# Merging VectorE calls in a convolution ahead of a GELU MLP, and leading with four short token blocks in place of six

## The chip, the cores and the metric

The kernel runs on one core of a Trainium2 chip. The metric is the time of one execution in device microseconds (us), taken as the median of several executions. The granted TensorE clock is the mean of a whole run. In four runs (two of the kernel before, one each of runs 2 and 4) it was 0.999 at ordinary times, and these count as undisturbed; a run at 1.000 or 0.999 is called clean.

## The reference, cut to what matters

A causal depthwise convolution of seven taps (softmax weights, one set for each of eight groups of 24 channels) is followed by a two-layer MLP with an exact GELU. Everything is float32 outside, bfloat16 in the matmuls.

```python
# x (8, 4096, 192), weight (8, 7), w_in (192, 2048), w_out (2048, 192)
w = softmax(weight, axis=-1)
x_pad = concat([zeros(B, 6, D), x], axis=1)          # causal: six zeros ahead of each sequence
a[b, s, c] = sum_k w[c // 24, k] * x_pad[b, s + k, c]
h = a.reshape(32768, 192) @ w_in
out = gelu_exact(h) @ w_out
```

## The kernel before

The 32768 tokens are two halves of 16384, worked on together; a block is so many tokens of both halves. `WS` gives the block sizes. For each block the following happens:

- SyncE loads the input into one of three buffers `xin`.
- VectorE transposes it to channel-major form (`xT`; 192 channels of two halves are three parts of 128 rows) and runs seven taps over it. The last tap writes `xc` in bfloat16.
- TensorE multiplies by `w_in` (here mm1) in slices: eight slices for a 256-token block, sixteen for one of 512. Each slice fills one of two PSUM buffers `hp`.
- ScalarE applies the GELU to a slice and frees its `hp` buffer. So TensorE can be two slices ahead of ScalarE, no more.
- TensorE multiplies the GELU's output of the block before by `w_out` (mm2), a share after each slice of mm1.

Blocks 0 and 1 are convolved on TensorE. For the blocks in `K0`, ScalarE takes the first tap (a scaled copy), at the slices that `first` names; it needs the transposed block for that. TensorE's program order is mm1 slice, mm2 share, mm1 slice, and so on, without any slack.

```python
    WS = [256] * 6 + [512] * ((HALF - 1536) // 512)
    PC = {0: 0, 1: 1}                # convolved on TensorE
    K0 = {4: 0, 5: 1, 6: 2}          # first tap on ScalarE
    NA = 5                           # blocks whose output ScalarE evacuates
    M0, M1 = 6, NB - 1               # first and last block of the transposed mm2
# ... (cut)
            def trans(n, p):                       # VectorE, part p of block n
                # ... waits for the input, for xT to be free, for the halo
                v.transpose(
                    ap(xT[n % 2], p * XW + HX, [[NP * XW, 128], [1, w]]),
                    ap(xin[n % NX], p, [[TB // 32 * DQ, 128], [D if n == 0 else DQ, w // 32], [NP, 32]]),
                ).then_inc(S_TR)

            def conv(n, k, p):                     # VectorE, tap k of part p
                # ... waits
                if k == h and h:
                    v.wait_ge(S_K0, NP * K0[n] + p + 1)
                elif idx >= NP:
                    v.wait_ge(S_CV, idx - NP + 1)
                src = ap(xT[n % 2], p * XW + HF + kt, [[NP * XW, 128], [1, w]])
                a = acc[n % 2][:, p * TB : p * TB + w]
                # k == 0: tensor_scalar; else scalar_tensor_tensor(dst, src, wk, a, mult, add)

            for n in range(2, NB):                 # VectorE's order
                ops = [] if n in K0 else [("t", n, p) for p in range(NP)]
                ops += [("c", n, k, p) for k in range(int(n in K0), KS) for p in range(NP)]
                if n + 1 in K0:
                    ops[9:9] = [("t", n + 1, p) for p in range(NP)]
                plan.append(ops)
# ... (cut) ScalarE
            for n, at in ((4, (3, 5, 6)), (5, (3, 5, 6)), (6, (2, 3, 5))):
                for p in range(NP):
                    first[n - 2, at[p]] = (n, p)   # ahead of slice at[p] of block n - 2
            for n in range(NB):
                for i in range(NSL[n]):
                    if (n, i) in first:
                        first_tap(*first[n, i])    # waits for S_TR of that part
                    for k in due.get((n, i), []):
                        evac(a, *k)
                    a.wait_ge(S_MM1, u + 1)        # u counts slices over all blocks
                    a.activation(out=..., in_=hp[u % 2], func=AF.Gelu).then_inc(S_GELU)
# ... (cut) TensorE
            def mm1(n, i):
                if u >= 2:
                    t.wait_ge(S_GELU, u - 1)       # the hp buffer is free
                if i == 0:                         # (blocks 0 and 1 wait for other semaphores: cut)
                    t.wait_ge(S_CV, cvd(n))        # the whole block is convolved
```

## Time and profile before

| | before |
|---|---|
| time, median of 4 runs | 682.59 us (682.43 to 682.80) |
| span of the profiled run, clock | 680.6 us, 1.000 |
| VectorE: busy, calls | 561.7 us, 906 |
| VectorE waiting for TensorE at the output transpose | 99.9 us |
| TensorE from block 4's first slice to block 6's (two short blocks) | 49.91 to 70.95 us |

TensorE is the bound (busy for 99% of the span, 98% of the chain of waits). The timeline of each engine gives the start of every call, and the difference of two starts is what a call costs its engine. The lines are in the prediction.

### The profile page before, as it was taken

To read this page: it belongs to the slowest core of one execution; us is meant where nothing else is said; L and a number is where in the kernel's file an instruction comes from. 1 tells how busy PE (TensorE), PEld (TensorE's weight loads), DVE (VectorE), ACT (ScalarE), POOL (GpSimd) and SP (SyncE) were. 2 spreads that over 40 slices of the span, in tenths; PEclk is the share of its full clock that TensorE was granted. 3 is DMA by queue.
4 is the path that set the end of the run, shared out by engine and by line. 5 is a ranking of instruction groups with operands and counts; after the bars stand their busy time and mean duration, and the time that the engine had idled before them with its cause. 6 is when DMAs were issued, how large, how long until landed. Compare 5 with 4: busy or idle time off the path is not lost.

```text
span 680.6 us, 27316 instructions
## 1 busy us (share of the span) xinstructions
PE 674.6 (99%) x12576; PEld 407.5 (60%) x12576; DVE 561.7 (83%) x906; ACT 536.5 (79%) x548; POOL 38.9 (6%) x57
## 2 busy tenths in 40 slices
PE   8999999999999999999999999999999999999998
PEld 4999655555555555555555555555555555555557
DVE  6999989888889888899888898888898888988611
ACT  6899987787787877787777788777778777778772
POOL 5126000000000000000000000000000000000000
PEclk9999999999999999999999999999999999999999
DMA  9446233134442133331244422334322444310123
GB/s 223 88 99 138 64 71 81 43 69 95 96 94 61 45 87 94 95 89 46 59 95 94 94 70 45 78 94 96 89 56 47 95 94 96 80 40 25 48 50 94
DMA packets 132994, 54.79 MB, mean 81 GB/s; under 512 B 126480, under 2 KB 132752, under 8 KB 132880
## 3 DMA queue, kind: packets, MB, share of 16 engines
q1 hardware_dynamic: 130960, 51.50, 32.6%
q8 instruction: 98, 1.61, 1.0%
q0 software_dynamic: 1248, 0.79, 0.9%
q10 hardware_dynamic: 672, 0.76, 0.4%
q14 instruction: 16, 0.13, 0.1%
HBM read 28.66 MB, written 25.17 MB: 79 GB/s over the span
## 4 chain that ended last, share of the span: by engine, by line
PE 98%; ACT 1%; DMA 1%; DVE 0%; SPq 0%; issue 0%; ACTq 0%
PE hp L763 48%; PE ob L823 43%; PE ob L793 5%; PE hp L793 1%; DMA xin<-in_x_dram 1%; ACT gT L684 1%; PE ob L714 0%; ACT xc L191 0%; DVE xT L529 0%; ACT xTb L633 0%; SPq L871 0%; DVE osb L283 0%; SPq L332 0%; ACTq L632 0%
## 5 line engine op out<-in xcount | busy, mean ns | idle before, releaser
L684 ACT ACTIVATE gT<-hp 128x1024 bf16<-128x1024 f32 x512 | 523.2, 1024 | 129.0 <-PE hp L763 125.7
L763 PE MATMUL hp<-xc,win 64*64 64x512 bf16 (+2 forms) x6048 | 418.6, 366 | 1.5 <-ACT gT L684 1.1
L823 PE MATMUL ob<-gT,wout 64*64 64x512 bf16 x5376 | 366.3, 376 | 0.0
L562 DVE SCALAR_TENSOR_TENSOR acc<-xT,wcol,acc 128x512 f32<-128x512 f32 (+1 forms) x495 | 314.5, 699 | 0.0
L763 PEld LDWEIGHTS hp<-xc,win 64*64 64x64 bf16 (+1 forms) x6048 | 187.6, 106 | 136.1 <-ACT gT L684 2.6
L823 PEld LDWEIGHTS ob<-gT,wout 64*64 64x64 bf16 x5376 | 172.1, 118 | 123.0
L314 DVE STREAM_TRANSPOSE osb<-ob 128x512 f32<-128x512 f32 x84 | 74.1, 885 | 99.9 <-PE ob L823 99.9
L529 DVE STREAM_TRANSPOSE xT<-xin 128x512 f32<-128x512 f32 (+1 forms) x105 | 78.5, 797 | 3.4 <-DMA xin<-in_x_dram 3.4
L562 DVE SCALAR_TENSOR_TENSOR xc<-xT,wcol,acc 128x512 bf16<-128x512 f32 (+1 forms) x99 | 65.1, 712 | 0.0
L450 POOL COPY xT<-xT 128x18 f32<-128x18 f32 x30 | 27.9, 929 | 505.3 <-DVE xT L529 483.0
L793 PE MATMUL ob<-wout,gT 64*128 64x192 bf16 x896 | 46.8, 243 | 0.0
L793 PEld LDWEIGHTS ob<-wout,gT 64*128 64x128 bf16 x896 | 38.6, 94 | 5.2 <-issue 0.4
L555 DVE TENSOR_SCALAR acc<-xT,wcol 128x512 f32<-128x512 f32 (+1 forms) x90 | 37.5, 473 | 1.1
L698 PE MATMUL hp<-warm 128*128 128x512 bf16 x16 | 5.5, 516 | 1.3 <-DVE warm L466 1.3
L285 ACT ACTIVATE osb<-ob 128x192 f32<-128x192 f32 x2 | 0.7, 331 | 7.1 <-PE ob L793 7.1
L793 PE MATMUL hp<-wout,gT 64*128 64x192 bf16 x128 | 5.9, 243 | 0.0
L283 DVE COPY osb<-ob 128x192 f32<-128x192 f32 x2 | 0.7, 358 | 6.1 <-PE ob L793 6.1
L793 PEld LDWEIGHTS hp<-wout,gT 64*128 64x128 bf16 x128 | 5.3, 94 | 0.0
L657 ACT ACTIVATE acc<-xT,wcol 128x256 f32<-128x256 f32 (+1 forms) x9 | 5.2, 575 | 0.0
L270 ACT ACTIVATE osb<-ob 128x384 f32<-128x384 f32 x10 | 4.9, 486 | 0.0
L698 PEld LDWEIGHTS hp<-warm 128*128 128x128 bf16 x16 | 1.9, 126 | 4.3 <-issue 2.5
L387 POOL DMA_DIRECT2D win<-in_moe_w_in_dram x6 | 3.9, 660 | 0.8 <-POOLq L904 0.8
(36 smaller groups left out, 31.4 us busy)
## 6 DMA issues: line engine op xcount, KB each, us to landing
out_dram<-osb SPq DMA_DIRECT2D x122, 192.0 KB, 3.1
xin<-in_x_dram SPq DMA_DIRECT2D x116, 192.0 KB, 4.1
xin<-in_x_dram SPq DMA_DIRECT2D x20, 96.0 KB, 4.3
woutf<-in_moe_w_out_dram SPq DMA_DIRECT2D x4, 384.0 KB, 5.9
win<-in_moe_w_in_dram POOLq DMA_DIRECT2D x4, 96.0 KB, 4.6
win<-in_moe_w_in_dram POOLq DMA_DIRECT2D x2, 192.0 KB, 5.1
out_dram<-osb SPq DMA_DIRECT2D x8, 48.0 KB, 1.7
out_dram<-osb ACTq DMA_DIRECT2D x4, 96.0 KB, 2.0
```

The source lines that it names most:

```text
L270: e.activation(out=dst, in_=src, func=AF.Copy).then_inc(S_EVA)
L314: v.transpose(ap(osb[m % 2], j, [[8 * C, 128], [C // 2, TB // 32], [NP, 32]]), bank(ring(m, j)),).then_inc(S_EV)
L450: g.tensor_copy(dst, src).then_inc(S_HALO)
L529: v.transpose(ap(xT[n % 2], p * XW + HX, [[NP * XW, 128], [1, w]]), ap(xin[n % NX], p, [[TB // 32 * DQ, 128], [D if n == 0 else DQ, w // 3 ...
L555: ins = v.tensor_scalar(a, src, wk, None, ALU.mult)
L562: ins = v.scalar_tensor_tensor(dst, src, wk, a, op0=ALU.mult, op1=ALU.add)
L657: a.activation(out=acc[n % 2][:, p * TB : p * TB + w], in_=ap(xT[n % 2], p * XW + HX, [[NP * XW, 128], [1, w]]), func=AF.Copy, scale=wcol[ ...
L684: a.activation(out=ap(gT[n % 2], i * c * 2 * w, dst), in_=ap(hp[u % 2], 0, src), func=AF.Gelu,).then_inc(S_GELU)
L698: t.matmul(hp[1][:, 0:512], warm[:, 0:128], warm[:, :])
L763: ins = t.matmul(hp[u % 2][fo : fo + fw, o : o + w], ap(win, f1, [[NP * F, 64], [2, fw]]), xc[n % 2][r, p * TB : p * TB + w], start=(p == ...
L793: ins = t.matmul(bb[sub], gT[m % 2][r, c0 : c0 + 128], wout[r, CH[sub][i] * C : (CH[sub][i] + 1) * C], start=(ph == 0 and i == 0), stop=(p ...
L823: ins = t.matmul(bank(ring(m, j), slice(64 * h, 64 * h + 64), w), ap(wout, 64 * hf * NF * C + CH[h][i] * C + j, [[NF * C, 64], [NP, 64]],) ...
```

## The change

The intent is to take work off VectorE (two calls for a tap instead of three, one transpose instead of three) and to reach the long blocks sooner with the margin that this gives. TensorE now waits for two thirds of a block before its first matmul and for the rest two matmul pairs later. The diff, cut to its core:

```diff
-    WS = [256] * 6 + [512] * ((HALF - 1536) // 512)
+    WS = [256] * 4 + [512] * ((HALF - 1024) // 512)
-    K0 = {4: 0, 5: 1, 6: 2}
-    NA = 5
+    K0 = {3: 0, 4: 1, 5: 2}
+    NA = 3
-    M0, M1 = 6, NB - 1
+    M0, M1 = 4, NB - 1
 # trans: for n >= 2 one call
+                    v.transpose(
+                        ap(xT[n % 2], HX, [[NP * XW, 128], [XW, NP], [1, w]]),
+                        ap(xin[n % NX], 0, [[TB // 32 * DQ, 128], [1, NP], [DQ, w // 32], [NP, 32]]),
+                    ).then_inc(S_TR)
 # conv: s is 0 (two parts) or 1 (one part)
+                p0, pn = (0, 2) if s == 0 else (2, 1)
-                src = ap(xT[n % 2], p * XW + HF + kt, [[NP * XW, 128], [1, w]])
+                src = ap(xT[n % 2], p0 * XW + HF + kt, [[NP * XW, 128], [XW, pn], [1, w]])
-                a = acc[n % 2][:, p * TB : p * TB + w]
+                a = ap(acc[n % 2], p0 * TB, [[NP * TB, 128], [TB, pn], [1, w]])
 # VectorE's order
-                    ops[9:9] = [("t", n + 1, p) for p in range(NP)]
+                    ops[6:6] = [("t", n + 1, 0)]
 # ScalarE's places for the first taps
-            for n, at in ((4, (3, 5, 6)), (5, (3, 5, 6)), (6, (2, 3, 5))):
+            for n, at in ((3, (5, 6, 7)), (4, (3, 5, 6)), (5, (2, 4, 6))):
 # TensorE
-                        t.wait_ge(S_CV, cvd(n))
+                        t.wait_ge(S_CV, cvd(n) - 1)     # and cvd(n) ahead of the last part
 # cut: semaphore counts, the places of evacuations on VectorE, and the waits of the first taps:
 # each now waits for the whole transposed block, and block 3's no longer for block 1's convolution
```

More of the change, by code (lines that the diff above doesn't have):

```diff
@@ L202, in wait_pc @@
                 e.wait_ge(S_PCE, 2 + (1, 3, 6)[p])
-        NCV = NP * KS
+        NCV = 2 * KS
         FQ = F // 8
@@ L216, in cast, with trd @@
             ).then_inc(S_CAST[PC[n]])
+        def trd(n):
+            return NP * (n + 1) if n < 2 else 2 * NP + n - 1
         def cvd(n):
-            return sum(NCV - NP * (m in K0) for m in range(n + 1) if m not in PC)
+            return sum(NCV - 2 * (m in K0) for m in range(n + 1) if m not in PC)
         HC = [0]
@@ L321, in load @@
             if n >= NX:
-                e.wait_ge(S_TR, NP * (n - NX + 1))
+                e.wait_ge(S_TR, trd(n - NX))
             for q in qs:
@@ L436, in halo @@
                     return
-                g.wait_ge(S_TR, NP * n)
+                g.wait_ge(S_TR, trd(n - 1))
                 if n == 1:
@@ L528, in trans @@
                         v.wait_ge(S_HALO, HC[n])
+                if n >= 2:
+                    v.transpose(
+                        ap(xT[n % 2], HX, [[NP * XW, 128], [XW, NP], [1, w]]),
+                        ap(
+                            xin[n % NX],
+                            0,
+                            [[TB // 32 * DQ, 128], [1, NP], [DQ, w // 32], [NP, 32]],
+                        ),
+                    ).then_inc(S_TR)
+                    return
                 v.transpose(
@@ L536, in trans, with conv @@
                 ).then_inc(S_TR)
-            def conv(n, k, p):
+            def conv(n, k, s):
                 w = WS[n]
                 h = int(n in K0)
-                if k == h and p == 0:
-                    v.wait_ge(S_TR, NP * (n + 1))
-                if k == 1 and p == 0:
+                p0, pn = (0, 2) if s == 0 else (2, 1)
+                if k == h and s == 0:
+                    v.wait_ge(S_TR, trd(n))
+                if k == 1 and s == 0:
                     v.wait_ge(S_HALO, HC[n + 1])
-                idx = cvd(n - 1) + NP * (k - h) + p
+                idx = cvd(n - 1) + 2 * (k - h) + s
                 kt = KS - 1 - k
                 if k == h and h:
-                    v.wait_ge(S_K0, NP * K0[n] + p + 1)
-                elif idx >= NP:
-                    v.wait_ge(S_CV, idx - NP + 1)
-                src = ap(xT[n % 2], p * XW + HF + kt, [[NP * XW, 128], [1, w]])
+                    v.wait_ge(S_K0, NP * K0[n] + p0 + pn)
+                elif idx >= 2:
+                    v.wait_ge(S_CV, idx - 1)
+                src = ap(xT[n % 2], p0 * XW + HF + kt, [[NP * XW, 128], [XW, pn], [1, w]])
                 wk = wcol[:, kt : kt + 1]
-                a = acc[n % 2][:, p * TB : p * TB + w]
+                a = ap(acc[n % 2], p0 * TB, [[NP * TB, 128], [TB, pn], [1, w]])
                 if k == 0:
@@ L558, in conv @@
                     if k == KS - 1:
-                        dst = xc[n % 2][:, p * TB : p * TB + w]
-                        if n >= 2 and p == 0:
+                        dst = ap(xc[n % 2], p0 * TB, [[NP * TB, 128], [TB, pn], [1, w]])
+                        if n >= 2 and s == 0:
                             v.wait_ge(S_MM1, SL0[n - 1])
@@ L570, in _ @@
             for n in range(2, NB):
-                ops = [] if n in K0 else [("t", n, p) for p in range(NP)]
-                ops += [("c", n, k, p) for k in range(int(n in K0), KS) for p in range(NP)]
+                ops = [] if n in K0 else [("t", n, 0)]
+                ops += [("c", n, k, q) for k in range(int(n in K0), KS) for q in range(2)]
                 if n + 1 in K0:
-                    ops[9:9] = [("t", n + 1, p) for p in range(NP)]
+                    ops[6:6] = [("t", n + 1, 0)]
                 plan.append(ops)
@@ L593, in _ @@
                 conv_out(v, 1, j)
-            side = [((M0 + 2, 7 * g), evac, v, M0 - 1, g) for g in range(NG[M0 - 1])]
+            side = [((M0 + 2, 4 * g), evac, v, M0 - 1, g) for g in range(NG[M0 - 1])]
             for n in range(M0, M1):
-                for j, at in enumerate([(n + 2, 18), (n + 3, 6), (n + 3, 9)]):
+                for j, at in enumerate([(n + 2, 12), (n + 3, 4), (n + 3, 6)]):
                     side.append((at, evac_t, v, n, j))
@@ L653, in first_tap @@
                 w = WS[n]
-                a.wait_ge(S_TR, NP * n + p + 1)
-                if p == 0:
+                a.wait_ge(S_TR, trd(n))
+                if p == 0 and n >= 4:
                     a.wait_ge(S_CV, cvd(n - 2))
@@ L752, in mm1 @@
                     for p in range(NP):
-                        if n in PC and i == 0 and cc == 0 and p == NP - 1:
-                            wait_pc(t, n, p)
+                        if i == 0 and cc == 0 and p == NP - 1:
+                            if n in PC:
+                                wait_pc(t, n, p)
+                            else:
+                                t.wait_ge(S_CV, cvd(n))
                         for hf in range(2):
```

## The prediction

> **What bounds the kernel now.** I read the page first: busy shares, then the chain of waits.
>
> ```profile
> PE 674.6 (99%) x12576; PEld 407.5 (60%) x12576; DVE 561.7 (83%) x906; ACT 536.5 (79%) x548; POOL 38.9 (6%) x57
> ...
> PE 98%; ACT 1%; DMA 1%; DVE 0%; SPq 0%; issue 0%; ACTq 0%
> ```
>
> TensorE (PE) is busy for 99% of the span and holds 98% of the chain. VectorE (DVE), which the change speeds up, has none of it. The list of waits says the same from the other side:
>
> ```profile
> ACT gT L684 <- PE hp L763: 125.7, 413, 1.0
> DVE osb L314 <- PE ob L823: 99.9, 30, 11.8
> ...
> PE hp L763 <- ACT gT L684: 1.1, 3, 0.5
> ```
>
> VectorE stands 99.9 us waiting for TensorE; TensorE waits 1.1 us for ScalarE (ACT), all within the first 19 us. So in the steady state a shorter VectorE call buys nothing, and the decision falls in the ramp, where VectorE's margin is thin. There I read the timelines engine by engine. VectorE before, at the start and around its first 512-token block:
>
> ```profile
> 20.62 0.88 DVE L555 TENSOR_SCALAR acc<-xT,wcol 128x256 f32<-128x256 f32 x3
> 21.42 6.02 DVE L562 SCALAR_TENSOR_TENSOR acc<-xT,wcol,acc 128x256 f32<-128x256 f32 x15
> 27.35 1.27 DVE L562 SCALAR_TENSOR_TENSOR xc<-xT,wcol,acc 128x256 bf16<-128x256 f32 x3
> ...
> 51.06 2.41 DVE L529 STREAM_TRANSPOSE xT<-xin 128x512 f32<-128x512 f32 x3
> 53.38 2.44 DVE L562 SCALAR_TENSOR_TENSOR acc<-xT,wcol,acc 128x256 f32<-128x256 f32 x6
> 55.72 1.29 DVE L562 SCALAR_TENSOR_TENSOR xc<-xT,wcol,acc 128x256 bf16<-128x256 f32 x3
> 56.90 10.04 DVE L562 SCALAR_TENSOR_TENSOR acc<-xT,wcol,acc 128x512 f32<-128x512 f32 x15
> 66.84 2.08 DVE L562 SCALAR_TENSOR_TENSOR xc<-xT,wcol,acc 128x512 bf16<-128x512 f32 x3
> ```
>
> ScalarE in block 2 and in block 4 before, where it computes the first taps (L657) of blocks 4 and 6 between its GELUs (L684) and evacuations (L270):
>
> ```profile
> 33.28 0.50 ACT L657 ACTIVATE acc<-xT,wcol 128x256 f32<-128x256 f32 x1
> 33.68 1.02 ACT L684 ACTIVATE gT<-hp 128x1024 bf16<-128x1024 f32 x1
> ...
> 53.01 0.71 ACT L657 ACTIVATE acc<-xT,wcol 128x512 f32<-128x512 f32 x1
> 53.62 1.01 ACT L684 ACTIVATE gT<-hp 128x1024 bf16<-128x1024 f32 x1
> ```
>
> The first tap of a block needs that block's transposed input, [...] a late transpose holds up the GELU behind the tap. Here both arrive just in time.
>
> [...]
>
> **The change, part by part.**
>
> *Call costs, start to start.* The two-input tap (SCALAR_TENSOR_TENSOR): 256 columns, (27.35-21.42)/15 = 0.395 us; 512 columns, (66.84-56.90)/15 = 0.663. So 256 columns cost 0.268 and a call 0.128. Estimate for 1024: 0.663+2x0.267 = 1.197. A two-call tap is then 1.197+0.663 = 1.860 against 3x0.663 = 1.988 (512 tokens), or 0.663+0.395 = 1.058 against 1.185 (256 tokens). Tensor_scalar: 256 columns (21.42-20.62)/3 = 0.267, 512 columns 0.40. Transposes: 512 columns (53.38-51.06)/3 = 0.773, 256 columns 0.43 from starts, so 0.085 is fixed; one call of 3x256 is 1.12 and of 3x512 is 2.155 (estimates).
>
> *Steady state.* A block saves 7x0.13 of taps and 2x0.085 of transposes, 1.07 us, so over some 30 blocks about 32 us of VectorE. None of it is on the path. Worth to the end: 0.
>
> *Fewer short blocks.* On TensorE, two 256-token blocks took 21.04 us (block 4 starts at 49.91, block 6 at 70.95). One full 512-token block takes 20.75 (86.68 to 107.43). One replaces the other: minus 0.29 us. The transition block (mm1 512 wide, mm2 of the short block before it) keeps its 15.7 us but comes as block 4. The matmul count of L763 stays 6048; L793 falls from 1024 to 768 and L823 rises from 5376 to 5568.
>
> *The ramp, replayed by hand with these durations.* The first input transpose of block 2 starts at 19.24 as before (its DMA ends then). Transpose 1.12+0.09 latency, first tap 0.67, six taps of 1.058, with block 3's transpose (1.12) inside: block 2 is ready at 28.59. TensorE wants it at 28.87, and now waits only for two thirds of it: no stall. First taps of block 3 have moved to block 1's last three slices; the transpose is ready at 24.0, so ScalarE finds it ready and its delay of 0.5 us is swallowed by the double buffer.
> Block 3: three taps to 31.76, then block 4's transpose, now 512 tokens: 31.76+2.155+0.09 = 34.0. ScalarE wants it at 33.3 for the tap ahead of slice 3 of block 2. That GELU starts at 34.64 instead of 33.68 and ends 35.66; TensorE may be two slices ahead, and reaches slice 5 at 35.44, so it waits till 35.71: 0.27. The 512-wide taps (0.61 to the next start, against 0.40) before slices 5 and 6 leave ScalarE no slack (0.61+0.91 per slice of 1.315) and cost 0.19 and 0.20. Block 3 starts at 40.05 instead of 39.39.
> Block 4 on VectorE: block 3 is done at 37.09, but the second and third first taps end at 37.6 and 39.1, so VectorE waits 0.53 and 0.32. Three taps of 1.860 end at 43.52, then block 5's transpose: 43.52+2.155+0.09 = 45.77. **Here is the loss:** block 5's first tap sits ahead of slice 2 of block 3, where ScalarE arrives at 43.25. It stands still for 2.5 us. The tap then takes 0.61, the GELU ends at 47.42, and TensorE, ready for slice 4 at 40.05+4x1.315 = 45.31, starts it at 47.47: 2.16 us lost. A further 0.18 goes at slice 6, where a tap and an evacuation share a slice. Block 4 starts at 52.91 instead of 49.91.
> After this VectorE is ahead: block 4 ready at 51.3, block 5 at 62.4 against 68.6 wanted, and every later block sooner relative to TensorE. The loss stops growing, and is not recovered, since TensorE has no slack.
> Sum: 0.27+0.39+2.16+0.18 = 3.00, less 0.29: **plus 2.7 us**. 682.6+2.7 = 685.3.
>
> **Rivals.** (a) *Nothing stalls, only the short blocks count*: 682.3. For it: the list of waits shows TensorE untouched after 19 us; the slots were moved by someone who looked. Against: the transpose of block 5 stands behind three 512-token taps, and I find no earlier time for it than about 44.9 even with both VectorE waits taken out. (b) *VectorE becomes the bound in the ramp*: if a call with a two-row pattern costs more than my line predicts, block 2 is late by that much, and the transposes of blocks 4 and 5 too; each us of VectorE lateness before 45.8 is about a us at the end. 5% slower calls add some 1 us: 686.3. Against: pattern rows are long (256 or 512 columns). (c) *The saved calls shorten the steady state*: some 32 us of VectorE would give up to 650. Against: the 99.9 us that VectorE already waits for TensorE, and 0% in the chain. (d) *Input DMA*: block 3's transpose is now wanted at 22.8 instead of 28.5. Its last load is issued at 15.3 and such loads landed in 5.5, so 20.8: 2 us of margin, hidden.
>
> **Range and chances.** The central sum is 685.3. The first 45 us of VectorE are some 24 us of calls at times extrapolated by a factor of two; 3% off either way is 0.7 us. Rival (a) pulls the low side and (b) the high; the three runs before spread by 0.4. I take 683.2 to 686.7. Two per cent is 13.7 us, and no mechanism but (c), or a ramp far worse than computed, gets there: within 2% with 0.98.
>
> **What would show it.** VectorE's calls fall from 906 to 600 (counted from the diff), its busy time by 25 to 40 us, and its wait for L823 grows by about as much. Taps of 128x1024 every 1.2 us. In the list of waits, first taps (L657's successor) on VectorE's transpose with a longest wait of 2 to 3 us near 43 to 46, and TensorE on GELU near 45 to 47, some 3 us in all. Wrong, if TensorE's gaps there are missing (time near 682.3), if gaps appear after 70 us, or if the steady block is not 20.75 us.

## The result, and the profile after

The changed kernel took 686.70 us (median of 4 runs: 686.21, 686.25, 687.15, 688.84) against 682.59. The ratio is 1.0061, 95% interval 1.0044 to 1.0078. Here and below the ratio of two kernels and its interval are those for the runs of the same rounds; they are not quite the ratio of the medians. Two of the four runs show a granted clock of 0.998; they are the two longest.

The page of the changed kernel, busy shares and chain:

```profile
PE 676.2 (99%) x12512; PEld 400.5 (58%) x12512; DVE 528.3 (77%) x600; ACT 535.9 (78%) x544; POOL 33.0 (5%) x56
...
PE 93%; DVE 3%; DMA 2%; ACT 1%; SPq 1%; issue 1%; POOL 0%; POOLq 0%
```

VectorE does the same work in 33.4 us less and in 600 calls. For the first time it has a share of the chain, 3%. The list of waits (who waited for whom; total, times, longest) says where:

```profile
DVE osb L318 <- PE ob L842: 134.2, 31, 11.8
...
PE hp L782 <- ACT gT L700: 3.6, 5, 2.0
ACT acc L673 <- DVE xT L534: 3.6, 2, 2.5
```

The VectorE time saved is now waiting: 99.9 us has become 134.2. The last line is new. Two first taps (L673) on ScalarE waited for VectorE's transpose, one of them 2.5 us. The timelines of ScalarE, VectorE and TensorE at that place (start, duration, in brackets the idle time before and what ended it):

```profile
34.49 0.72 ACT L673 ACTIVATE acc<-xT,wcol 128x512 f32<-128x512 f32 x1 [1.03 <-DVE xT L534]
...
46.25 0.72 ACT L673 ACTIVATE acc<-xT,wcol 128x512 f32<-128x512 f32 x1 [2.53 <-DVE xT L534]
46.88 1.92 ACT L700 ACTIVATE gT<-hp 128x1024 bf16<-128x1024 f32 x2
```

```profile
38.16 5.89 DVE L578 SCALAR_TENSOR_TENSOR acc<-xT,wcol,acc 128x1024 f32<-128x1024 f32 x6 [0.55 <-ACT acc L673]
43.96 2.25 DVE L534 STREAM_TRANSPOSE xT<-xin 128x1536 f32<-128x1536 f32 x1
```

```profile
44.47 0.82 PE L782 MATMUL hp<-xc,win 64*128 64x256 bf16 x12
45.13 0.82 PE L812 MATMUL ob<-wout,gT 64*128 64x192 bf16 x16
47.94 0.84 PE L782 MATMUL hp<-xc,win 64*128 64x256 bf16 x12 [1.99 <-ACT gT L700]
48.61 1.45 PE L812 MATMUL ob<-wout,gT 64*128 64x192 bf16 x16
49.85 1.49 PE L782 MATMUL hp<-xc,win 64*128 64x256 bf16 x12
51.13 1.27 PE L812 MATMUL ob<-wout,gT 64*128 64x192 bf16 x16
52.24 0.82 PE L782 MATMUL hp<-xc,win 64*128 64x256 bf16 x12
```

VectorE finishes three 512-token taps of block 4 at 43.96 and only then transposes block 5. ScalarE has come to block 5's first tap 2.5 us before and stands still, with two filled slices behind it: their GELUs start only behind the tap, at 46.88. TensorE runs out of `hp` buffers for 1.99 us. (The bracket counts from the modelled end of the matmul before, so a loss read from two starts is some 0.17 us more.) Then comes something that the prediction did not have: the two slices after the gap take 1.91 and 2.39 us (47.94 to 49.85, 49.85 to 52.24) instead of 1.31. The table by stretches has the granted clock as the third number from the right:

```profile
46.00:48.00 2.00, 0.06 (x2) 0.07 (x4) 2.00 (x4) 1.75 (x3) 0.00 (x0) 1.00 1.15 204
48.00:50.00 2.00, 2.00 (x30) 1.89 (x32) 2.00 (x4) 2.00 (x4) 0.00 (x0) 0.66 0.05 7
50.00:52.00 2.00, 2.00 (x26) 1.62 (x23) 2.00 (x3) 1.32 (x2) 0.17 (x1) 0.50 0.30 98
52.00:55.00 3.00, 3.00 (x66) 2.83 (x64) 2.91 (x4) 2.62 (x4) 1.02 (x1) 0.99 0.02 5
```

Finer stretches put the half clock between 48.6 and 52.0 us: it set in 0.7 us after the gap had ended and lasted 3.4 us.

### The profile page after: what moved, and what is told of

Same layout as the page of the kernel before. It is cut to its first block, busy times and chain, and to the rows that moved or that the text cites. A ratio compares the mean times of both kernels' runs of the same rounds, so it can differ in the third digit from the quotient of the medians. Undisturbed runs are those within 1.5% of the kernel's fastest.

```text
span 685.3 us, 26864 instructions
## 1 busy us (share of the span) xinstructions
PE 676.2 (99%) x12512; PEld 400.5 (58%) x12512; DVE 528.3 (77%) x600; ACT 535.9 (78%) x544; POOL 33.0 (5%) x56
## 4 chain that ended last, share of the span: by engine, by line
PE 93%; DVE 3%; DMA 2%; ACT 1%; SPq 1%; issue 1%; POOL 0%; POOLq 0%
PE hp L782 46%; PE ob L842 44%; PE ob L812 2%; DVE acc L578 2%; DVE xT L534 1%; DMA xin<-in_x_dram 1%; PE hp L812 1%; DMA win<-in_moe_w_in_dram 1%; SPq L336 1%; ACT gT L700 1%; ACT acc L673 0%; SPq L896 0%; POOL win L391 0%; DVE xc L578 0%; DVE acc L571 0%
## 5 line engine op out<-in xcount | busy, mean ns | idle before, releaser
L842 PE MATMUL ob<-gT,wout 64*64 64x512 bf16 x5568 | 379.8, 376 | 0.0
L578 DVE SCALAR_TENSOR_TENSOR acc<-xT,wcol,acc 128x1024 f32<-128x1024 f32 (+1 forms) x320 | 295.2, 979 | 0.8 <-ACT acc L673 0.6
L842 PEld LDWEIGHTS ob<-gT,wout 64*64 64x64 bf16 x5568 | 178.3, 118 | 127.3
L318 DVE STREAM_TRANSPOSE osb<-ob 128x512 f32<-128x512 f32 x87 | 76.9, 887 | 134.2 <-PE ob L842 134.2
L534 DVE STREAM_TRANSPOSE xT<-xin 128x1536 f32<-128x1536 f32 (+1 forms) x32 | 71.8, 2244 | 1.7 <-DMA xin<-in_x_dram 1.7
L578 DVE SCALAR_TENSOR_TENSOR xc<-xT,wcol,acc 128x1024 bf16<-128x1024 f32 (+1 forms) x64 | 60.5, 990 | 0.0
L454 POOL COPY xT<-xT 128x18 f32<-128x18 f32 x29 | 22.0, 758 | 514.4 <-DVE xT L534 487.3
L812 PE MATMUL ob<-wout,gT 64*128 64x192 bf16 x640 | 34.7, 248 | 0.0
L571 DVE TENSOR_SCALAR acc<-xT,wcol 128x512 f32<-128x512 f32 (+2 forms) x58 | 33.0, 610 | 1.0
L812 PEld LDWEIGHTS ob<-wout,gT 64*128 64x128 bf16 x640 | 28.5, 96 | 4.9 <-issue 0.4
L673 ACT ACTIVATE acc<-xT,wcol 128x512 f32<-128x512 f32 (+1 forms) x9 | 5.9, 651 | 3.6 <-DVE xT L534 3.6
```

The source lines that it names most:

```text
L318: v.transpose(ap(osb[m % 2], j, [[8 * C, 128], [C // 2, TB // 32], [NP, 32]]), bank(ring(m, j)),).then_inc(S_EV)
L454: g.tensor_copy(dst, src).then_inc(S_HALO)
L534: v.transpose(ap(xT[n % 2], HX, [[NP * XW, 128], [XW, NP], [1, w]]), ap(xin[n % NX], 0, [[TB // 32 * DQ, 128], [1, NP], [DQ, w // 32], [NP ...
L571: ins = v.tensor_scalar(a, src, wk, None, ALU.mult)
L578: ins = v.scalar_tensor_tensor(dst, src, wk, a, op0=ALU.mult, op1=ALU.add)
L673: a.activation(out=acc[n % 2][:, p * TB : p * TB + w], in_=ap(xT[n % 2], p * XW + HX, [[NP * XW, 128], [1, w]]), func=AF.Copy, scale=wcol[ ...
```

## The experiments

Each was run five times (one of them six), in the same rounds and on the same chip as the kernel before, to which its ratio refers.

**1. The changed kernel once more.** No edit. Its purpose was the spread, and a trace at clock 1.000.

> The changed kernel once more, for its spread and a second trace. Its first four runs came in two kinds: 687.15 and 688.84 us with a granted clock of 0.998, 686.21 and 686.25 with 1.000. Theory A (a TensorE gap near 46 us that is 2.0 us long sometimes lets the clock fall to half for some 3.4 us): the runs again split, those at clock 0.998 or below are 1 to 2 us longer, and a trace at clock 1.000 has no slice of half clock. Rival B (the clock has no part, the spread is from the input DMA in the first 20 us): times and clocks do not go together. In both the wait of the first tap on the transpose near 44 us is again about 2.5 us, and the mean is 3.6 to 5.5 us above before.

It took 686.28 us (685.52 to 687.41), ratio 1.0057 (1.0044 to 1.0069). The two runs at clock 0.998 took 687.41 and 687.20, the three at 1.000 took 685.52, 685.90 and 686.28. The profiled run had clock 1.000, with the same wait of 2.53 us and the same gap:

```profile
44.73 0.82 PE L782 MATMUL hp<-xc,win 64*128 64x256 bf16 x12
45.39 0.82 PE L812 MATMUL ob<-wout,gT 64*128 64x192 bf16 x16
48.20 0.83 PE L782 MATMUL hp<-xc,win 64*128 64x256 bf16 x12 [1.99 <-ACT gT L700]
48.87 0.82 PE L812 MATMUL ob<-wout,gT 64*128 64x192 bf16 x16
49.52 0.82 PE L782 MATMUL hp<-xc,win 64*128 64x256 bf16 x12
```

The same gap of 1.99 us was followed by the half clock in one trace and not in the other. Times and clocks go together, as theory A had it. This clean trace is the one to hold the prediction's sum against.

**2. Only the places of block 5's first taps on ScalarE.**

```diff
-            for n, at in ((3, (5, 6, 7)), (4, (3, 5, 6)), (5, (2, 4, 6))):
+            for n, at in ((3, (5, 6, 7)), (4, (3, 5, 6)), (5, (5, 6, 7))):
```

> Only the place of block 5's three first taps on ScalarE moves, from slices 2, 4, 6 of block 3 to slices 5, 6, 7. Theory A (the order of ScalarE's queue makes the loss): the 2.5 us wait of the tap goes, the 2.0 us gap of TensorE and the half clock behind it go, block 4 starts at about 51.2 us instead of 54.9; taps close to block 4 leave ScalarE 0.4 to 0.6 us behind, which block 4 has no slack for. So 683.3 to 684.2 us, some 3 us under the changed kernel. Rival C (VectorE is the bound in the ramp, whatever ScalarE does): TensorE then waits for block 4 on VectorE instead and the time stays at 686 to 687.

It took 683.87 us (683.69 to 684.57), ratio 1.0021 (1.0009 to 1.0034). The 2.5 us wait and the gap are gone from the trace, and TensorE started block 4 at 51.76 us instead of 53.66 in run 1. So three numbers in ScalarE's order are worth 2.4 us by the medians, with VectorE's work untouched: 1.9 us of it at block 4's start in the two clean traces, the rest in the runs at half clock, of which this version has none. Rival C falls for that part.

**3. The merged calls alone**: the changed kernel with `WS`, `K0`, `NA`, `M0` and the places of before.

```diff
-    WS = [256] * 4 + [512] * ((HALF - 1024) // 512)
-    K0 = {3: 0, 4: 1, 5: 2}
+    WS = [256] * 6 + [512] * ((HALF - 1536) // 512)
+    K0 = {4: 0, 5: 1, 6: 2}
 # and NA = 5, M0 = 6, first taps at (4, (3, 5, 6)), (5, (3, 5, 6)), (6, (2, 3, 5))
```

> Six leading 256-token blocks as before, with before's places of the first taps, but two-call taps and one transpose per block. Theory A: merged calls are off the path and cost nothing: 682.3 to 682.9 us, VectorE busy near 528 us, its wait for TensorE above 130 us. Rival D (the merged transpose, which is ready only as a whole, holds up ScalarE by itself): 684 us or more with a wait of a first tap on the transpose of over 1.5 us.

It took 682.21 us (682.14 to 683.12), ratio 0.9999 (0.9985 to 1.0012). VectorE was busy 528.1 us and waited 129.8 us for TensorE. Taking 33.6 us of busy time off an engine that is not the bound changed nothing that can be measured here.

**4. The four short blocks alone**: the kernel before with `WS`, `K0`, `NA`, `M0` and the places of the changed kernel, calls and transposes in threes.

```diff
-    WS = [256] * 6 + [512] * ((HALF - 1536) // 512)
-    K0 = {4: 0, 5: 1, 6: 2}
+    WS = [256] * 4 + [512] * ((HALF - 1024) // 512)
+    K0 = {3: 0, 4: 1, 5: 2}
 # and NA = 3, M0 = 4, first taps at (3, (5, 6, 7)), (4, (3, 5, 6)), (5, (2, 4, 6)),
 # and block 3's first tap without the wait for block 1's convolution
```

> Before's three-call taps and three transposes, with four leading 256-token blocks and the changed kernel's places of the first taps. Theory A: the loss is of the block sizes and places: the first tap of block 5 waits about 2 us near 44 to 46 us, and besides block 2 is late on VectorE by about 1 us, so 685.5 to 688 us, like the whole change. Rival D (the loss comes from the merged calls): 682.5 to 683.5 us.

It took 686.30 us (685.64 to 686.79), ratio 1.0053 (1.0041 to 1.0066). The first tap of block 5 waited 2.3 us, and TensorE stood still for 1.59 us at block 2 (late on VectorE) and for 1.80 us at the slice behind that tap. None of its five runs had a clock of 0.998. The loss belongs to the block sizes with these places, not to the merged calls.

**5. Block 5 wholly on VectorE.**

```diff
-    K0 = {3: 0, 4: 1, 5: 2}
+    K0 = {3: 0, 4: 1}
-            for n, at in ((3, (5, 6, 7)), (4, (3, 5, 6)), (5, (2, 4, 6))):
+            for n, at in ((3, (5, 6, 7)), (4, (3, 5, 6))):
```

> The changed kernel, but block 5 has its first tap and its transpose on VectorE in the ordinary order, so ScalarE never waits for block 5. Theory A: the 2.5 us wait and the 2.0 us gap go, with nothing given back in block 4 (no first taps late in block 3); the 0.9 us lost to block 4's first taps stays. TensorE starts block 4 at about 51.3 us in the profile; 683.5 us (683.1 to 684.0), clock 1.000 in all runs. Rival C (VectorE bounds the ramp): block 5 is late on VectorE and the time stays above 685.

It took 683.90 us (683.41 to 684.23), ratio 1.0013 (1.0001 to 1.0026), all clocks 1.000. The long wait is gone; block 4's own wait, 0.8 us here, stays.

**6. Blocks 4 and 5 wholly on VectorE.**

```diff
-    K0 = {3: 0, 4: 1, 5: 2}
+    K0 = {3: 0}
-            for n, at in ((3, (5, 6, 7)), (4, (3, 5, 6)), (5, (2, 4, 6))):
+            for n, at in ((3, (5, 6, 7)),):
```

> The same for blocks 4 and 5: only block 3 keeps its first taps on ScalarE. Theory A: no tap waits on a transpose any more, block 4 is ready on VectorE at about 50.2 us, just when TensorE comes to it; 682.2 to 682.9 us, even with before, perhaps 0.3 under. Rival C: VectorE, with the two first taps more (2.1 us), is late for block 4 or 5 and TensorE waits for it by 1 us or more: above 683.5.

It took 682.52 us (681.96 to 683.00), ratio 0.9993 (0.9981 to 1.0006). Giving VectorE more work, the two first taps, took away the whole loss. What is left of TensorE's waits in the ramp is 0.42 us for block 2:

```profile
29.68 0.92 PE L782 MATMUL hp<-xc,win 64*128 64x256 bf16 x12 [0.42 <-DVE xc L578]
```

That rules rival C out as the cause of the loss.

**7. The transposes ahead of the taps**, ScalarE's order as in the changed kernel.

```diff
                 if n + 1 in K0:
-                    ops[6:6] = [("t", n + 1, 0)]
+                    q = 0 if n in K0 else 6
+                    ops[q:q] = [("t", n + 1, 0)]
```

> The changed kernel, with only the place of two VectorE calls moved: the transposes of blocks 4 and 5 come before the taps of blocks 3 and 4 and no longer behind three of them. ScalarE's queue stays as it is. Theory A (the transpose's place behind 512-token taps makes the wait): both waits of first taps on transposes (1.0 and 2.5 us) go, and the 2.0 us gap with them; block 4 is ready on VectorE at about 50.6 us, 0.5 us after TensorE comes to it; 682.8 to 683.6 us, clock 1.000. Rival C (VectorE's work as a whole is too long for the ramp, the order only moves the wait): 685 us or more, with TensorE waiting for block 4 or 5 by over 2 us.

It took 683.86 us (683.47 to 685.02), ratio 1.0016 (1.0003 to 1.0029), all clocks 1.000. No first tap waits any more; the one wait of TensorE that the list of waits still names is at block 4, for VectorE. The timelines of VectorE and of TensorE, one line each:

```profile
38.63 2.30 DVE L534 STREAM_TRANSPOSE xT<-xin 128x1536 f32<-128x1536 f32 x1 [0.60 <-DMA xin<-in_x_dram]
```

```profile
51.53 0.96 PE L783 MATMUL hp<-xc,win 64*128 64x512 bf16 x6 [1.16 <-DVE xc L578]
```

The median is 0.26 us above the range expected, and the two lines show why: the transpose of block 5 now comes so early that it waits 0.60 us for its input, and block 4 is late by that much more, 1.16 us where 0.5 was expected. So there is a bit of rival C in it: with block 5's transpose ahead of it, block 4 is a real deadline for VectorE.

**8. Block 4's input load held back.** VectorE started block 2 later in the traces with four short blocks (19.62, 19.86, 20.09, 20.25 us) than in the first two with six (19.24, 19.50).

```diff
             if n >= NX:
-                e.wait_ge(S_TR, trd(n - NX))
+                e.wait_ge(S_TR, trd(2) if n == 4 else trd(n - NX))
```

> The changed kernel, with the input load of block 4 (twice as large since the change) held back until block 2 is transposed. VectorE started block 2 at 19.24 and 19.50 us in the traces with six short blocks, at 19.62, 19.86, 20.09 and 20.25 with four. Theory E (block 4's larger load slows block 2's): block 2 starts at 19.2 to 19.5 us, and every later step of the ramp comes 0.4 to 0.6 us sooner: 685.3 to 686.0 us. Rival (jitter of the start): block 2 starts at 19.6 us or later and the time stays near 686.3.

It took 686.53 us (685.61 to 687.87), ratio 1.0059 (1.0045 to 1.0072), the same as without it. Block 2 started at 19.59 us, the three runs at clock 1.000 took 685.61 to 686.53, the two at 0.998 took 687.54 and 687.87. The run does not support theory E. Three later traces with six short blocks started block 2 at 19.42, 19.70 and 21.30 us, so the start moves from run to run by itself. In each of these traces VectorE waits for block 2's own input before that start, 1.48 us here and 2.32 us in run 9's; what moves the landing stays open. The seven traces with four short blocks and the load as it was lie between 19.62 and 20.45 us, the two with the load held back (this one and run 12's) at 19.59 and 19.68, so a small share of the larger load is neither shown nor excluded.

**9, 10, 11. A TensorE gap without the change.** In the kernel before, copies into an unused buffer are put on ScalarE ahead of slice 2 of block 3. The results stay right. Run 9 has two copies of 1600 columns, run 10 two of 1820, run 11 three of 1440.

```diff
+                    if (n, i) == (3, 2):
+                        for q in range(4):
+                            a.wait_ge(S_WOUT[q], 16)
+                        for q in range(2):
+                            a.activation(out=pad[:, 1600 * q : 1600 * q + 1600],
+                                         in_=woutf[:, 0:1600], func=AF.Copy)
```

> The kernel before, with 3.1 us of copies into an unused buffer put on ScalarE ahead of slice 2 of block 3: a TensorE gap alone, made without VectorE. By the double buffer TensorE should stand still for about 2.0 us near 44.5 us. Theory A2 (a gap of 2 us after the dense work of the ramp can let the clock fall to half): some runs have a clock of 0.998 and 1.2 to 1.8 us more, so 684.6 in the clean runs and 686 in the others. Rival (the half clock needs what else the change brings): all runs at clock 1.000 and 684.6 us.

> As the run with 3.1 us of copies on ScalarE in the kernel before, but with 0.34 us more of them: the TensorE gap, 1.59 us there, should be 1.9 to 2.0 us, as long as in the changed kernel. If a gap of 2.0 us alone can halve the clock, some of the five runs show 0.998 and are 1.2 to 1.8 us longer than the rest (685.2 in the clean ones); if the length is not what matters, [...]all five have clock 1.000.

> The same with 3.9 us of copies: a TensorE gap of about 2.6 us. Time 685.9 where the clock holds. Theory A2: the longer gap halves the clock more often than in the changed kernel (6 of 14 runs so far), so in three or more of five runs, 0.998 and 1.2 to 1.8 us more. Rival (the half clock has nothing to do with the gap): all runs at 1.000.

| | gap in the trace | median | ratio | runs at clock 0.998 |
|---|---|---|---|---|
| run 9 | 1.59 us | 684.93 us | 1.0030 (1.0018 to 1.0043) | 0 of 5 |
| run 10 | 1.96 us | 685.40 us | 1.0033 (1.0021 to 1.0045) | 0 of 5 |
| run 11 | 2.62 us | 687.22 us | 1.0061 (1.0045 to 1.0077) | 4 of 6 |

In run 9 the gap came out shorter than expected; in the profiled run block 2 was 0.87 us late besides. In run 11 the four runs at 0.998 took 687.13 to 689.49 us, the two at 1.000 took 685.21 and 685.96. Its trace, by stretches:

```profile
46.00:48.00 2.00, 0.00 (x0) 0.00 (x0) 1.71 (x5) 2.00 (x3) 0.20 (x1) 1.00 0.36 64
48.00:50.00 2.00, 1.92 (x32) 1.77 (x34) 0.49 (x1) 2.00 (x5) 0.00 (x0) 0.75 0.00 0
50.00:52.00 2.00, 2.00 (x24) 1.68 (x22) 0.48 (x1) 1.73 (x3) 0.00 (x0) 0.50 0.29 98
52.00:54.00 2.00, 2.00 (x42) 1.89 (x39) 1.25 (x4) 1.48 (x3) 0.00 (x0) 0.89 0.03 8
```

This is the picture of the changed kernel, made with nothing but a longer gap in the kernel before. A gap of 2.62 us alone is enough for the half clock, and whether it comes differs from run to run. Run 10, with the changed kernel's gap length, met it in none of five runs, where the changed kernel (run 8's variant included) met it in 6 of 14. Run 4, with a gap of 1.80 us, had none in five either. Whether that difference is chance or the shorter waits around the gap in the changed kernel is not settled.

**12. Runs 6 and 8 together**, as the best version that the experiments point to.

> The changed kernel with blocks 4 and 5 wholly on VectorE and block 4's input load held back until block 2 is transposed. Theory A: nothing in the ramp waits; what remains is the 0.29 us of the fewer short blocks, and the jitter of block 2's input, which the later load may take some of (19.59 us in the one trace of it). 682.0 to 682.7 us, clock 1.000 in all runs, so at best 0.5 us under before. Rival E2 (block 2's start is jitter that the later load leaves alone): even with the run without the later load, 682.5, and a start of block 2 anywhere from 19.2 to 20.5 us.

It took 682.35 us (682.07 to 683.22), ratio 0.9986 (0.9973 to 1.0000). From 26 us on, the list of waits names none of TensorE in the ramp. The kernel before was slower than usual on this chip (683.60 median of 9). The interval touches 1, so this is the best of the versions, but a gain is not shown beyond doubt. The 0.29 us that the prediction gave to fewer short blocks is smaller than the interval and stays unconfirmed by a time.

## Why the prediction was right or wrong

The mechanism and the sign were right, and the size was too small: plus 2.7 us predicted, plus 4.1 measured (686.70 less 682.59): at the very edge of the range, and beyond it in half of the runs. Point by point:

- **The steady state is worth 0.** Right (run 3). VectorE's busy time fell by 33.4 us and its wait for TensorE rose by 34.3.
- **The costs of the merged calls.** Right. A two-call tap of 512 tokens: ten calls from 51.69 to 61.15 us are 1.892 us a tap, estimate 1.860. The transpose of 3x512 took 2.19 us start to start (32.18 to 34.37), estimate 2.155; that of 3x256 1.14, estimate 1.12. So 768 elements more of a transpose cost 1.05 us, 1.37 ns each, and a two-call tap came 1.7% above the estimate. What makes up the 0.128 us that a call costs beside its columns, no run shows.
- **Where the largest loss is.** Right: block 5's first tap waited 2.53 us for the transpose (predicted 2.5). Starts of slices in the clean trace of run 1 give the terms. The wait at slice 4 of block 3 is 44.73 to 48.20 less a slice of 1.315, which is 2.16 (predicted 2.16). Those around block 4's second and third first taps are 0.18 and 0.21 (0.19 and 0.20), that at slice 6 of block 3 is 0.19 (0.18).
- **The first step that failed is the start.** "The first input transpose of block 2 starts at 19.24 as before" was one trace's number taken for a constant. Over all the traces the start lies between 19.24 and 21.30 us; it was 19.86 in the clean trace of the changed kernel. TensorE started block 2 at 29.09 (not 28.87), its first slice took 0.10 us longer than a normal one, and the wait at slice 5 was 0.67 where 0.27 was predicted. So slice 5 started at 36.43 where the sum had 35.71, 0.72 us later: 0.62 is the later start, and 0.10 is calls and latencies on the way. The other traces bear this out. In all five that keep the changed kernel's order up to there (block 2 at 19.59, 19.62, 19.86, 20.09 and 20.29 us) slice 5 came 16.56 or 16.57 us after the start; the sum had 16.47. TensorE started block 4 at 53.66, 3.75 us later than in the kernel before, where the sum had 3.00. With six short blocks there was more room: in the trace of run 9 block 2 started 2.06 us later than in the first trace, and TensorE stood still for 0.87 us at block 2 and for nothing behind it but the gap made on purpose. Now the first taps behind it are deadlines as thin.
- **The second is the clock.** No clock loss was put in the sum. The trace before could not show one: its clock is 1.000, and the longest of TensorE's three waits for the GELU is 0.5 us (1.1 in all), where the sum loses 2.16 at one slice. That such a gap costs its length alone was the estimate. Here the clock halved for some 3.4 us behind a gap of 1.99 us in the first trace, and 6 of 14 runs of the changed kernel and its run-8 variant had a clock of 0.998; behind one of 2.62 us (run 11) it was 4 of 6, and with 1.59, 1.80 and 1.96 us in three other kernels (runs 9, 4 and 10) 0 of 15. The mean of the six is 687.67 us, that of the other eight 686.02: 1.65 us. In the first trace the two slow slices, 1.91 and 2.39 us, are 1.67 over two normal ones. Averaged over the runs it is some 0.7 us.
- **Together**: clean runs are 3.4 us above before (686.02 less 682.6), where the sum had 2.7. The start (0.6) and the slightly longer calls and latencies (0.1) make up the difference, in the one clean trace of this kernel itself; the clock adds 0.7 on average, 1.65 when it comes.
- **The rivals.** (a), no stall, fell: it needs runs 6 or 12, not the change. (b), VectorE as the bound of the ramp, was right in one respect: its lateness at block 2 goes on to TensorE one for one, as the five traces show, though nearly all of it came from the start and not from the calls. (c) fell with run 3. (d), input DMA, was dismissed for block 3's load, rightly (no wait there), but block 2's load sets the start of the whole chain, and how much that start moves was not asked.

## What to carry to other kernels

A call placed in another engine's in-order queue makes its producer's order part of that engine's deadline (block 5's first tap stood 2.53 us on ScalarE): when a block doubles in size, every hand-placed slot behind it has to be worked out again, and here three slot numbers were worth 2.4 us. On a kernel whose bound engine is full (TensorE was busy for 99% of the span here), look for the places where the others are only just ahead, and count on the time lost there not coming back: run 1 came to block 4 3.75 us late, and its span was 3.6 us longer (684.2 against 680.6). TensorE gaps of 1.96 and 2.62 us (runs 10 and 11) cost 2.6 and 2.8 us in the runs at clock 1.000. Behind gaps of 1.99 and 2.62 us part of the runs, those at 0.998, took another 1.65 and 2.3 us through the half clock.
